# A channel MLP on one core: an inner Strassen level on four instead of two products of matmul 2, with seeded PSUM banks and weight sums kept in DRAM

## The chip, the cores and the metric

The kernel runs on one core of a Trainium2 chip. The metric is the device time of one execution in microseconds (us). Engines are named as in the profile: PE is TensorE (PEld its weight loads), DVE is VectorE, ACT is ScalarE, POOL is GpSimd, and SP is SyncE, whose queue issues nearly all DMAs.

## The reference

```python
B, S, D, F = 1, 2048, 1024, 3584          # all inputs bf16

def reference(x, w1, b1, w2, b2):
    y = _layernorm(x, axis=-1)            # (x - mean) / sqrt(var + 1e-5)
    h = _gelu(jnp.einsum("bsd,df->bsf", y, w1) + b1)    # tanh form
    return jnp.einsum("bsf,fd->bsd", h, w2) + b2
```

## The kernel before

The 2048 rows are done as two blocks (`s`) of 1024. A block is a layer norm of 8 tiles of 128 rows, a transposition into `yw_sb`, matmul 1 with the GELU into `h_sb`, and matmul 2 into the output.

Both matmuls use Strassen's algorithm in Winograd's form: operands are cut into 2 x 2 quarters, and seven products of sums of quarters take the place of eight. The sums of the left operand are called S1 to S4, those of the right T1 to T4, and the products 1 to 7: 1 is A11 B11, 2 is A12 B21, 3 is S4 B22, 4 is A22 T4, 5 is S1 T1, 6 is S2 T2, 7 is S3 T3. The result is C11 = 1 + 2; with U = 1 + 6: C12 = U + 5 + 3, C21 = U + 7 + 4 and C22 = U + 7 + 5. (The signs of the sums are chosen so that nothing but additions is left.)

**Matmul 1** (`mm1_unit`, L527) goes over 7 chunks of `w1` (three buffers in `w1_sb`), each of two units; a unit is 7 products of 4 matmuls with 512 columns (L548). The first chunk of the first block is done plainly (`mm1_plain`, L510), while x is still coming in. The w1 sums (L485) and the adds (`fin`, L565) are on DVE; copies of partial results (`snap`, L560) are on ACT or DVE; the GELU (L571) is on ACT. Output 11 of a unit is made as: product 1 is copied from its bank to SBUF (`o1`), product 2 goes to a bank of its own (`bp2`), DVE adds them (`c11`), ACT applies the GELU to the sum.

**Matmul 2** (`mm2_block`, L627) contracts over 28 tiles of 128, so a quarter of it has `NU` = 14. Products run in the order `SEQ2 = (1, 2, 5, 3, 6, 7, 4)`. A plain product (`prods`, L681) is 4 row tiles x 14 matmuls of 512 columns. Products 2 and 4 have a second Strassen level inside (`inner`, L733): seven sub-products of 14 matmuls with 256 columns, in the order 1, 5, 6, 2, 7, 3, 4, whose operand sums (8 per product, two DVE operations each) are written into space that is free then: `t1_sb` and `w1_sb` for product 2, `h` quarters 12 and 11 for product 4. All evictions of matmul 2 are DVE adds (L645), which add `b2` or an earlier result and leave a snapshot in `sn_sb` (12 slots) or an output tile in `o_sb`. The sums S1 to S4 and T1 to T4 of matmul 2 are made by DVE in each block (`sums`, L618): S over h quarters in place, T over the w2 quarters in place. The w2 quarters 11 and 21 lie in `w2a_sb`, 12 and 22 in `yw_sb`, where matmul 1's y operands were; they are loaded in each block.

**The order of work** is not written by hand. Each operation is an `Op` with a cost, dependencies, a due time (`prio`) and slots of a pool (8 PSUM banks, 12 snapshots, output buffers), and a planner (`Planner.place`, L101) places them on the engines one after the other: on each engine, among operations that can start within a small slack, the one with the earliest due time. This fixes the order in each engine's queue; on the chip the queues run in order and wait on semaphores. DMAs are planned as one server of 350 KB/us with 2.1 us of latency. The loads, output stores and the transposes by DMA (`dma_T`, L432) are issued on SP. The layer norm of block 1 (`ln`, L366) is statistics and scaling on DVE, with the power on POOL; three tiles of the head's layer norm run on ACT (`ln_act`, L383).

Of the kernel before, what the change touches and what calls it, by code (L numbers as in the profile page):

```python
# [6 lines left out]
ALU = mybir.AluOpType  # L7
# [16 lines left out]
P = 128  # L24
# [4 lines left out]
N_OUT = 6  # L29
N_WARM = 26  # L30
OPEN_JOBS = 5
LN_ACT = (2, 4, 6)
# [12 lines left out]
class Op:  # L45
    __slots__ = ("engs", "cost", "fn", "deps", "prio", "sem", "inc", "nbytes", "alloc", "frees", "eng", "start",
                 "end", "n", "order", "name", "waiting", "users", "slot", "ready")

    def __init__(self, engs, cost, fn, deps, prio, name, sem=None, inc=1, nbytes=None, alloc=None, frees=()):
        self.engs = (engs,) if isinstance(engs, str) else tuple(engs)  # L50
        self.cost, self.fn, self.prio, self.name = cost, fn, prio, name
        self.deps = [d for d in deps if d is not None]
        self.sem, self.inc, self.nbytes, self.frees = sem, inc, nbytes, frees
        self.alloc = () if alloc is None else alloc if isinstance(alloc, tuple) else (alloc,)
        self.eng = None
        self.start = self.end = 0.0
        self.n = 0
        self.slot = None


class Slots:

    def __init__(self, n):
        self.free = [(k, None) for k in range(n)]


class Holder:


    def __init__(self, pool):  # L70
        self.pool = pool
        self.k = None


class Planner:
# [13 lines left out]
    @staticmethod  # L89
    def take(alloc):  # L90

        n, res = {}, []
        for h in alloc:
            i = n.get(id(h.pool), 0)
            if i >= len(h.pool.free):
                return None
            res.append(h.pool.free[i])
            n[id(h.pool)] = i + 1
        return res

    def place(self):  # L101
# [12 lines left out]
        while left:  # L114
            best = None
            for e in self.ENGS:
                cands = []
                t0 = 1e9
                for o in avail:
# [6 lines left out]
                    for _, rel in slots:  # L126
                        if rel is not None:
                            r = max(r, rel.end + LAT)
# [15 lines left out]
            for h, (k, rel) in zip(o.alloc, self.take(o.alloc)):  # L144
                h.k = k
                if rel is not None:
                    o.deps.append(rel)
            for h in o.alloc:
                h.pool.free.pop(0)
# [8 lines left out]
            for h in o.frees:  # L158
                h.pool.free.append((h.k, o))
                h.pool.free.sort(key=lambda f: f[1].end if f[1] is not None else 0.0)  # L160
            order[e].append(o)
            for u in o.users:
                u.waiting -= 1
                u.ready = max(u.ready, o.end + (LAT if u.engs != (e,) else 0.06))
# [45 lines left out]
def bass_standalone__mixer_channel_mlp__prompt_kernel(  # L210
# [24 lines left out]
    with ExitStack() as es:  # L235
# [11 lines left out]
        b2_sb = sb("b2_sb", [P, D], BF16)  # L247
        b1r_sb = sb("b1r_sb", [FT, P], BF16)
# [23 lines left out]
        w2q = {11: w2a_sb[:, 0], 21: w2a_sb[:, 1], 22: quarter(yw_sb, 0), 12: quarter(yw_sb, 1)}  # L272
        w2q16 = {11: w2a16[:, 0], 21: w2a16[:, 1], 22: quarter(yw16, 0), 12: quarter(yw16, 1)}
# [13 lines left out]
        T_MM2 = TH * 5 * NU * MM512 + 2 * 7 * NU * MM256  # L287
# [30 lines left out]
        w2_ld = {}  # L318

        def load_w2(s, q, deps, prio):  # L320
            w2_ld[(s, q)] = dma(w2q[q], w2v[:, q // 10 - 1, :, (q % 10 - 1) * HT:(q % 10) * HT], deps, prio,
                                f"w2_{s}_{q}", f"w2_{q}", NU * P * HT * 2)


# [23 lines left out]
        def warm(n, deps, prio):  # L348
            hold = Holder(banks)
# [5 lines left out]
        hold_b = Holder(banks)  # L355
# [50 lines left out]

        y_in = {}
# [4 lines left out]
        def pe_T(s, i, prio):  # L412
            x_free[(s, i)], y_in[(s, i)] = [], []
            for k in range(2):
                hold = Holder(banks)
# [111 lines left out]
        def mm1_unit(s, c, v, T, t0):  # L527
# [3 lines left out]
            b0, bp2, bp5 = Holder(banks), Holder(banks), Holder(banks)  # L531
            hold = {1: b0, 6: b0, 7: b0, 4: b0, 5: bp5, 3: bp5, 2: bp2}
# [5 lines left out]
            def prod(p, deps):  # L538
# [4 lines left out]
                first = p in (1, 2, 5)  # L543
# [12 lines left out]
            def snap(p, o, hold_s, at):  # L556
                hb = hold[p]
                def fn(e):
                    src, dst = ps[:, hb.k, :], sn_sb[:, hold_s.k, :]
# [19 lines left out]
            o1 = snap(1, P1, s1, pt[6] - SLOT)  # L579
            P5 = prod(5, ())  # L580
            o5 = snap(5, P5, s5, pt[3] - SLOT)
            P6 = prod(6, (P1, o1))
            o2 = snap(6, P6, s2, pt[7] - SLOT)
            P2 = prod(2, ())
            c11 = fin(2, P2, o1, s1, pt[2] + 4 * SLOT, (bp2,))
            gelu(11, sn(s1), c11, pt[2] + 6 * SLOT, (s1,))
# [4 lines left out]
            c12 = fin(3, P3, o2, s2, pt[3] + 4 * SLOT, (bp5,))  # L591
# [10 lines left out]
        w2_free = {}  # L602
        SLOT2 = NU * MM512
        SEQ2 = (1, 2, 5, 3, 6, 7, 4)
        INNER = (2, 4)
        KI = NU // 2
        HI = HT // 2

        def sums(dst, a, b, op, deps, prio, name, step=2, cost=0.63):
# [3 lines left out]
            for g, k0 in enumerate(range(0, n, step)):  # L613
                k1 = min(k0 + step, n)
                dl = list(deps)
                for k in range(k0, k1):
                    dl += a[1][k] + b[1][k]
                o = add("DVE", cost * (k1 - k0) / step, lambda e, k0=k0, k1=k1: e.tensor_tensor(  # L618
                    out=dst[:, k0:k1, :], in0=a[0][:, k0:k1, :], in1=b[0][:, k0:k1, :], op=op),
                    list(dict.fromkeys(dl)), prio + 0.15 * step * g, f"{name}_{g}")  # L620
                res += [[o]] * (k1 - k0)
# [5 lines left out]
        def mm2_block(s):  # L627
            t0 = base2[s]
            pt = {}
            for p in SEQ2:  # L630
                pt[p] = t0
                t0 += 7 * NU * MM256 if p in INNER else TH * SLOT2
            m2, rd, sn = {}, {}, {}
            hb = [Holder(banks) for _ in range(TH)]
            h5 = [Holder(banks) for _ in range(TH)]
            hold = {1: hb, 6: hb, 7: hb, 5: h5, 3: h5}
            prev = {1: None, 5: None, 6: 1, 7: 6, 3: 5}
            A = {q: (h[q], [[h_ok[(s, q, u)]] for u in range(NU)]) for q in h}
            B = {q: (w2q[q], [[w2_ld[(s, q)]]] * NU) for q in w2q}

            def done(p):
                return m2[p] if p in INNER else [m2[(p, t)] for t in range(TH)]

            def plus(out, bank, x):
                return lambda e: e.tensor_tensor(out=out(), in0=bank(), in1=x(), op=ALU.add)  # L645

            def bias(d):
                return lambda: b2_sb[:, d * HT:(d + 1) * HT]

            def whole(t, h_):  # L650
                return lambda: t[:, h_.k, :]

            def keep(p, t, d, at):
                hs = sn[(p, t)] = Holder(snaps)
                rd[(p, t)] = add("DVE", 0.69, plus(whole(sn_sb, hs), whole(ps, hold[p][t]), bias(d)),
                                 (m2[(p, t)], b2_ld), at, f"r{p}_{s}_{t}", alloc=hs)

            def store(q, t, ho, deps, at):
                r = (s * NT + (q // 10 - 1) * TH + t) * P
                c = (q % 10 - 1) * HT  # L660
                add("SP", 0.42, lambda e: e.dma_start(of[r:r + P, c:c + HT], o_sb[:, ho.k, :]), deps, at + 0.5,
                    f"st{q}_{s}_{t}", sem=ho, inc=16, nbytes=P * HT * 2, frees=(ho,))

            def final(p, t, q, add_p, at, frees, kept=False):

                ho, hs = Holder(outs), sn[(add_p, t)]
                bank = whole(ps, hold[p][t])
                fn = [(plus(whole(o_sb, ho), bank, whole(sn_sb, hs)), ())]
                alloc = (ho,)
                if kept:  # L670
                    hk = sn[(p, t)] = Holder(snaps)
                    fn.append((plus(whole(sn_sb, hk), bank, bias(0)), ()))
                    alloc += (hk,)
                f = rd[(p, t)] = add("DVE", 0.65 * len(fn), fn, (m2[(p, t)], rd[(add_p, t)], b2_ld), at,
                                     f"o{q}_{s}_{t}", alloc=alloc, frees=(hs, *frees))
                store(q, t, ho, (f,), at)

            def prods(p, a, b):
                first = prev[p] is None
                for t in range(TH):  # L680
                    fn = [(lambda e, k=k, t=t: e.matmul(  # L681
                        ps[:, hold[p][t].k, :], lhsT=a[0][:, k, t * P:(t + 1) * P], rhs=b[0][:, k, :],
                        start=(first and k == 0), stop=(k == NU - 1), skip_group_check=True), a[1][k] + b[1][k])
                        for k in range(NU)]
                    dl = [] if first else [rd[(prev[p], t)]]
                    for _, dd in fn:
                        dl += dd
                    m2[(p, t)] = add("PE", NU * MM512, fn, list(dict.fromkeys(dl)), pt[p] + t * SLOT2, f"M{p}_{s}_{t}",
                                     alloc=hold[p][t] if first else None)
                    at = pt[p] + (t + 1) * SLOT2  # L690
                    if p in (1, 5, 6):
                        keep(p, t, 0 if p == 1 else 1, at)
                    if p == 6:
                        final(3, t, 12, 6, at + 1, (h5[t],))
                    if p == 7:
                        final(7, t, 22, 5, at, (hb[t],), kept=True)

            def inner(p, a, b, xb, yb, war, q, add_p):
# [6 lines left out]
                SUB = 2 * KI * MM256  # L705
                at = {r: pt[p] + k * SUB for k, r in enumerate(SEQ1)}

                def tt(dst, x, y, op, r, n):
                    return sums(dst, x, y, op, war, at[r] - 3 * SUB, f"i{n}_{nm}", step=4, cost=0.62)

                s1 = tt(xb[0], X["21"], X["22"], ALU.add, 5, "S1")
                t1 = tt(yb[0], Y["12"], Y["11"], ALU.subtract, 5, "T1")
                s2 = tt(xb[1], s1, X["11"], ALU.subtract, 6, "S2")
                t2 = tt(yb[1], Y["22"], t1, ALU.subtract, 6, "T2")
                s3 = tt(xb[2], X["11"], X["21"], ALU.subtract, 7, "S3")
                t3 = tt(yb[2], Y["22"], Y["12"], ALU.subtract, 7, "T3")
                s4 = tt(xb[3], X["12"], s2, ALU.subtract, 3, "S4")
                t4 = tt(yb[3], Y["21"], t2, ALU.subtract, 4, "T4")
# [191 lines left out]
```

## Time and profile before

| | |
|---|---|
| median of 6 runs | 353.19 us (351.96 to 353.67) |
| the profiled execution | 353.12 us |
| its span | 351.3 us, granted TensorE clock 1.00 |
| busy shares | PE 98%, DVE 81%, ACT 36%, PEld 53% |
| DMA | 40.98 MB, mean 117 GB/s |
| matmul 1 of block 0 | 29.65 to 99.6 us of the span (after the first chunk, done plainly) |
| matmul 2 of block 0 | 99.6 to 181 us |
| matmul 1 of block 1 | 181 to 266 us |
| matmul 2 of block 1 | 266 to 347.9 us |

The span is the time from the first to the last instruction in the profile; what the device time has beyond it lies ahead of it and behind. The profile comes from one execution. A line of the chain in order of time gives start, duration, engine, tile and source line, and the number of instructions; consecutive instructions of one line are merged. A few matmul records are missing from the trace, so a count can be low by some. In a line of the groups, "busy, mean" is followed by the idle time ahead of the instructions on their engine, with what ended it.

### The profile page before, as it was taken

How to read it: one execution, taken by the hardware profiler on the slowest of the kernel's cores; microseconds unless marked ns; L12 is line 12 of the kernel's file. 1: busy time of each engine (PE TensorE's matmuls, PEld its weight loads, DVE VectorE, ACT ScalarE, POOL GpSimd, SP SyncE). 2: the span in 40 equal slices, each digit the busy share in tenths (PEclk: the TensorE clock that was granted, in tenths of full speed). 3: DMA queues.
4: the chain of work that ended last, by engine and by line, in shares of the span. 5: the costliest groups of instructions: out<-in, count | busy, mean ns of one | idle time of the engine just before them, and what ended most of it. 6: DMA issues, size and time to landing. Idle time of an engine off the chain costs nothing.

```text
span 351.3 us, 5124 instructions
## 1 busy us (share of the span) xinstructions
PE 342.8 (98%) x2003; PEld 185.9 (53%) x2011; DVE 284.6 (81%) x509; ACT 124.9 (36%) x200; POOL 12.2 (3%) x31
## 2 busy tenths in 40 slices
PE   4999999999999999999999999999999999999996
PEld 4986444444445754444765444444444675444475
DVE  4688899798789998999997557656448999797993
ACT  3765766677630000000025677667763000000000
POOL 2220010001100000000000000000000000000000
PEclk9999999999999999999999999999999999999999
DMA  7648929700057057055656432130005701001101
GB/s 243 237 62 300 327 55 356 250 0 3 0 176 244 30 126 264 19 103 109 186 186 205 155 119 75 48 119 0 2 0 197 223 30 33 0 0 47 45 30 62
DMA packets 47394, 40.98 MB, mean 117 GB/s; under 512 B 12298, under 2 KB 45322, under 8 KB 47370
## 3 DMA queue, kind: packets, MB, share of 16 engines
q1 hardware_dynamic: 47226, 40.52, 37.6%
q8 instruction: 16, 0.26, 0.3%
q10 hardware_dynamic: 144, 0.13, 0.2%
q14 instruction: 8, 0.07, 0.1%
HBM read 33.82 MB, written 4.19 MB: 108 GB/s over the span
## 4 chain that ended last, share of the span: by engine, by line
PE 96%; DMA 1%; ACT 1%; SPq 0%; issue 0%; DVE 0%; DVEq 0%
PE ps L548 45%; PE ps L681 34%; PE ps L733 12%; PE ps L510 4%; DMA x_sb<-in_x_dram 1%; PE ps L416 1%; ACT h_sb L387 0%; SPq L293 0%; ACT yw_sb L423 0%; DVE o_sb L645 0%; DVEq L235 0%; ACT mv_sb L389 0%; PE ps L356 0%
## 5 line engine op out<-in xcount | busy, mean ns | idle before, releaser
L548 PE MATMUL ps<-yw_sb,t_sb 128*128 128x512 f16 x416 | 96.3, 379 | 0.0
L560 ACT COPY sn_sb<-ps 128x512 f32<-128x512 f32 x65 | 38.1, 587 | 102.7 <-PE ps L548 102.7
L548 PE MATMUL ps<-yw_sb,w_sb 128*128 128x512 f16 x312 | 73.9, 379 | 0.0
L681 PE MATMUL ps<-yw_sb,h_sb 128*128 128x512 f16 (+1 forms) x332 | 73.0, 379 | 0.2
L548 PEld LDWEIGHTS ps<-yw_sb,t_sb 128*128 128x128 f16 x416 | 40.7, 98 | 48.6
L565 DVE TENSOR_TENSOR sn_sb<-ps,sn_sb 128x512 f32<-128x512 f32 x78 | 52.5, 688 | 15.3 <-PE ps L548 14.7
L571 ACT ACTIVATE h_sb<-sn_sb,b_sb 128x512 f16<-128x512 f32 x78 | 55.2, 719 | 25.1 <-DVE sn_sb L565 21.0
L681 PEld LDWEIGHTS ps<-yw_sb,h_sb 128*128 128x128 f16 x336 | 32.8, 98 | 38.8
L548 PEld LDWEIGHTS ps<-yw_sb,w_sb 128*128 128x128 bf16 x312 | 30.4, 98 | 36.0
L681 PE MATMUL ps<-w2a_sb,h_sb 128*128 128x512 f16 (+1 forms) x220 | 48.5, 379 | 0.2
L618 DVE TENSOR_TENSOR h_sb<-h_sb 128x1024 f16<-128x1024 f16 x72 | 45.3, 669 | 0.0
L681 PEld LDWEIGHTS ps<-w2a_sb,h_sb 128*128 128x128 f16 x224 | 21.9, 98 | 26.4
L645 DVE TENSOR_TENSOR o_sb<-ps,sn_sb 128x256 bf16<-128x256 f32 (+1 forms) x48 | 23.0, 509 | 5.4 <-PE ps L733 4.5
L485 DVE TENSOR_TENSOR t_sb<-w_sb,t_sb 128x1024 f16<-128x1024 bf16 x26 | 17.9, 688 | 11.1 <-PE ps L548 9.0
L645 DVE TENSOR_TENSOR sn_sb<-ps,b_sb 128x512 f32<-128x512 f32 x32 | 22.0, 686 | 5.9 <-PE ps L681 5.7
L485 DVE TENSOR_TENSOR t_sb<-w_sb 128x1024 f16<-128x1024 bf16 x26 | 17.8, 683 | 9.4 <-DMA w_sb<-in_w_dram 5.1
L368 DVE BATCH_NORM_STATS2 st_sb<-x_sb 128x6 f32<-128x512 bf16 x26 | 17.2, 680 | 4.8 <-DMA x_sb<-in_x_dram 4.8
L571 ACT ACTIVATE h_sb<-ps,b_sb 128x512 f16<-128x512 f32 x26 | 17.7, 682 | 1.9 <-PE ps L548 1.9
L510 PE MATMUL ps<-yw_sb,w_sb 128*128 128x128 f16 x256 | 16.7, 227 | 0.8 <-ACT yw_sb L423 0.8
L733 PE MATMUL ps<-w2a_sb,h_sb 128*128 128x256 f16 (+1 forms) x140 | 16.9, 273 | 0.0
L510 PEld LDWEIGHTS ps<-yw_sb,w_sb 128*128 128x128 bf16 x256 | 15.8, 102 | 1.5 <-DMA w_sb<-in_w_dram 1.0
L733 PEld LDWEIGHTS ps<-w2a_sb,h_sb 128*128 128x128 f16 x140 | 13.7, 98 | 2.7
(54 smaller groups left out, 207.1 us busy)
## 6 DMA issues: line engine op xcount, KB each, us to landing
w_sb<-in_w_dram SPq DMA_DIRECT2D x28, 512.0 KB, 6.6
w2a_sb<-in_w_dram SPq DMA_DIRECT2D x4, 1792.0 KB, 8.7
yw_sb<-in_w_dram SPq DMA_DIRECT2D x4, 1792.0 KB, 9.8
out_dram<-o_sb SPq DMA_DIRECT2D x32, 128.0 KB, 1.8
x_sb<-in_x_dram SPq DMA_DIRECT2D x15, 256.0 KB, 7.6
yw_sb<-x_sb SPq DMA_TRANSPOSE x20, 2.5
b_sb<-in_b_dram SPq DMA_DIRECT2D x1, 256.0 KB, 6.4
x_sb<-in_x_dram ACTq DMA_DIRECT2D x1, 128.0 KB, 2.8
```

The source lines that it names most:

```text
L368: st = [add("DVE", 0.68, lambda e, k=k: e.bn_stats(st_sb[:, i, 6 * k:6 * k + 6], x_sb[:, i, k * HT:(k + 1) * HT]), (x_ld[(s, i)][k], *gate ...
L416: fn = [(lambda e, j=j, k=k, hold=hold: e.transpose(out=ps16[:, hold.k, j * P:(j + 1) * P], in_=x16[:, i, k * HT + j * P:k * HT + (j + 1) ...
L485: return add("DVE", 0.65, lambda e: e.tensor_tensor(out=tv(k), in0=x0, in1=x1, op=ALU.subtract), [*deps, *war.get(k, ())], prio + 0.5 * k, ...
L510: fn = [(lambda e, b=b, hb=hold[f], f=f, k=k, t=t: e.matmul(ps[:, hb.k, t * P:(t + 1) * P], lhsT=lhs[:, k, f * P:(f + 1) * P], rhs=yop[f"A ...
L548: fn = [(lambda e, k=k: e.matmul(ps[:, hold[p].k, :], lhsT=lhs[:, k, :], rhs=yop[yo][:, k, :], start=(first and k == 0), stop=(k == KH - 1 ...
L560: return e.copy(out=dst, in_=src) if o_.eng == "ACT" else e.tensor_copy(dst, src)
L565: return add("DVE", 0.69, lambda e: e.tensor_tensor(out=sn_sb[:, hold_s.k, :], in0=ps[:, hold[p].k, :], in1=sn_sb[:, hold_s.k, :], op=ALU. ...
L571: r = h_ok[(s, q, u)] = add("ACT", 0.70, lambda e: e.activation(out=h[q][:, u, :], in_=src(), func=ACT.Gelu_apprx_tanh, bias=b1_sb[:, f:f ...
L618: o = add("DVE", cost * (k1 - k0) / step, lambda e, k0=k0, k1=k1: e.tensor_tensor(out=dst[:, k0:k1, :], in0=a[0][:, k0:k1, :], in1=b[0][:, ...
L645: return lambda e: e.tensor_tensor(out=out(), in0=bank(), in1=x(), op=ALU.add)
L681: fn = [(lambda e, k=k, t=t: e.matmul(ps[:, hold[p][t].k, :], lhsT=a[0][:, k, t * P:(t + 1) * P], rhs=b[0][:, k, :], start=(first and k == ...
L733: fn = [(lambda e, k=k, j=j: e.matmul(ps[:, bank[r].k, j * HI:(j + 1) * HI], lhsT=x[0][:, k, j * P:(j + 1) * P], rhs=y[0][:, k, :], start= ...
```

## The change

- **Products.** Matmul 2 runs its products in the order 5, 1, 2, 6, 3, 7, 4, and products 1, 2, 3 and 4 have the inner level (two plain products of 56 matmuls with 512 columns become 98 matmuls with 256 columns in each block). The inner sums are one DVE operation of 7 x 256 elements each, and share buffers from product to product: a buffer is written again when the sub-product of the product before that read it is done.
- **Seeds.** ScalarE copies a sum or a bias into a PSUM bank first, and the matmuls accumulate onto it: the difference of the two halves of b2 (`dl_sb`) under product 5, b2 under the sub-products 1 and 5 of product 1, product 1's result under product 6 and under sub-product 2 of product 2, and so on. Many evictions turn from DVE adds into ACT copies; the others are DVE adds of 128 x 512.
- **Matmul 1.** From the third chunk of block 0 on (`fork`), product 1 is copied from its bank into another PSUM bank, onto which product 6 accumulates, and product 2 accumulates onto product 1's own bank. The add `c11` on DVE goes; the GELU of output 11 reads PSUM.
- **w2 sums.** T1 to T4 are made once, in matmul 1 of block 0, in seven groups: two raw pieces of 256 KB are loaded into the free `x_sb`, DVE makes the four sums, and four stores of 256 KB write them to a DRAM tensor (`w2_sums`). Matmul 2 of each block loads T1 to T4 from there into the slots A to D and an h quarter (H), each when what it held is done with. The load of T1 in block 0 waits for the whole preparation.
- **Layer norm of block 1.** All of its passes are on ACT, the small operations on POOL (`ln_act2`); x of block 1 is loaded when the preparation has left `x_sb`.
- The planner takes account of the time at which a matmul inside an operation needs its dependency, and can hand out contiguous groups of slots.

The core of the diff, cut:

```diff
+SEQ2 = (5, 1, 2, 6, 3, 7, 4)
+INNER = ((1, 2, 3, 4), (1, 2, 3, 4))
...
+            fork = n > 1
+            b1, b0, b5 = Holder(banks), Holder(banks, seeded=True), Holder(banks)
+            hold = {1: b1, 2: b1, 6: b0, 7: b0, 4: b0, 5: b5, 3: b5}
...
-            o1 = snap(1, P1, s1, pt[6] - SLOT)
+            o1 = snap(1, P1, b0 if fork else s1, pt[6] - SLOT)
...
-            P2 = prod(2, ())
-            c11 = fin(2, P2, o1, s1, pt[2] + 4 * SLOT, (bp2,))
-            gelu(11, sn(s1), c11, pt[2] + 6 * SLOT, (s1,))
+            P2 = prod(2, (o1,) if fork else ())
+            if fork:
+                gelu(11, lambda: ps[:, b1.k, :], P2, pt[2] + 4 * SLOT, (b1,))
...
+        def w2_prep(ldA, ldB, gate, prio, dt):
...
+            for g in range(NU // PU):
+                u = slice(g * PU, (g + 1) * PU)
...
+                ld = [dma(raw(e), w2v[:, e, u, HT:2 * HT], [*war(e), *gate], at + 0.1 * e, f"pw{g}_{e}", f"pw{base + e}",
+                          PU * P * HT * 2) for e in range(2)]
...
+                T1 = tt(0, raw(0), A11[:, u, :], (ld[0], ldB), at + 3)
+                T2 = tt(1, raw(1), t16(0), (ld[1], T1), at + 3.5)
+                T3 = tt(2, t16(1), A11[:, u, :], (T2, ldB, *war(2)), at + 4)
+                T4 = tt(3, A21[:, u, :], t16(1), (T2, ldA, *war(3)), at + 4.5)
+                for j, T in enumerate((T1, T2, T3, T4)):
+                    st = dma(tq[j, :, u, :], t16(j), (T,), at + 5 + 0.1 * j, f"ps{g}_{j}", f"ps{base + j}", PU * P * HT * 2)
...
+            def inner(p, a, b, xb, yb, war, O=None, bias=None, out=None, gate=()):
...
+                    return sums(dst, x, y, op, war.get((n[0], r), ()), at[r] - 3 * SUB, f"i{n}{r}_{nm}", step=KI)
...
+                sd = copy(lambda: bank_q(c2), lambda: quart(g, 0, 0), (ok[11], subs[1]), at[1], f"s2_{nm}", alloc=c2)
+                k1 = copy(lambda: sn_sb[:, kk.k, :], lambda: ps[:, c0.k, :], (subs[1],), end(1), f"k1_{nm}", alloc=kk)
+                k5 = dve(lambda e: plus(e, quart(g, 1, 1), bank_q(c5), quart(g, 1, 1)), (subs[5], ok[22]), end(5), f"k5_{nm}")
+                sub(6, (k1,))
+                k2 = dve(lambda e: plus(e, quart(g, 0, 1), bank_q(c0), quart(g, 0, 1)), (subs[6], ok[12]), end(6), f"k2_{nm}")
+                sub(2, (sd,))
...
+            M5 = plain(5, S1, B[5], h5, False, [(o,) for o in sd5])
...
+            g1, ok1, sub1 = inner(1, A[11], B[1], X0, Y0, war0, gate=(M5[2],), bias=(
+                b2_sb[:, None, 0:HI].to_broadcast([P, 2, HI]), e0_sb[:, None, :].to_broadcast([P, 2, HI])))
...
+            sub2 = inner(2, A[12], B[2], X0, Y0, war_of(sub1), O=(g1, okw), out=11)
...
+            M6 = plain(6, S2, B[6], hb, False, [(o,) for o in sdb])
...
+            sub3 = inner(3, S4, B[3], X0, Y0, war_of(sub2), O=(g12, {11: O12[1], 12: O12[1], 21: O12[3], 22: O12[3]}), out=12)
...
+            M7 = plain(7, S3, B[7], hb, False, [(o,) for o in O12])
...
-                if s == 0 and c == 2:
-                    for q in (11, 21):
-                        load_w2(0, q, (jobs[-1],), t0 + 20 * SLOT)
+                if s == 0 and c == 1:
+                    gate = (w1_use[0][-1],)
+                    t21 = load_w2(0, "A", "B21", gate, t0 + 20 * SLOT)
+                    t11 = load_w2(0, "B", "B11", gate, t0 + 20 * SLOT + 0.1)
+                    prep = w2_prep(t21[1][0][0], t11[1][0][0], gate, t0 + 22 * SLOT, 5.5)
+            if s == 0:
+                W = {5: load_w2(0, "A", "T1", prep, base2[0] - 10), 1: t11}
...
-                    load_x(s + 1, i, [*x_free[(s, i)], *(head_end if s == 0 else ())], base1[s] + 40 + i)
-                    ln(s + 1, i, base2[s] + 10 + 4 * i)
+                    load_x(s + 1, i, [*x_gate[i]], base2[s] - 4 + i)
+                    ln_act2(s + 1, i, base2[s] + 10 + 5 * i, wf["ring"])
```

## The prediction

> **What bounds the kernel now.** I read the busy shares, the chain that ended last in order of time, the waits, the stretches by window, then the timeline of VectorE (DVE) for the pace of its sums.
>
> ```profile
> PE 342.8 (98%) x2003; PEld 185.9 (53%) x2011; DVE 284.6 (81%) x509; ACT 124.9 (36%) x200; POOL 12.2 (3%) x31
> PEclk9999999999999999999999999999999999999999
> ```
>
> TensorE (PE) is busy for all but the first 8.6 us and the last 3.4 us of the span, at the full granted clock. The chain says whether it ever waits inside.
>
> ```profile
> 99.63 10.74 PE ps L681 x49
> ...
> 111.67 9.17 PE ps L733 x84
> 120.84 3.02 PE ps L681 x14
> 123.86 1.53 PE ps L733 x14
> ...
> 337.15 10.71 PE ps L733 x98
> 347.88 0.42 DVE o_sb L645
> ```
>
> The chain is matmuls (96%). Four times 14 matmuls 512 wide is a plain product: 4 x 3.02 = 12.08 us. 98 matmuls 256 wide is a product with an inner level: 7 x 1.53 = 10.71 us, also at the very end, where no other product could be slipped between its steps. So the inner level runs without a gap, and any matmul taken away is time taken away, as long as what feeds TensorE keeps up. What that leaves is in the windows (us; then busy us of PE, PEld, DVE, ACT, POOL; clock; DMA share; GB/s) and the waits.
>
> ```profile
> 29.65:64.00 34.35, 34.35 (x160) 15.54 (x159) 31.02 (x53) 23.43 (x38) 1.48 (x2) 1.00 0.81 268
> 64.00:99.60 35.60, 35.58 (x165) 16.17 (x165) 29.12 (x57) 24.21 (x39) 3.30 (x6) 1.00 0.12 38
> 99.58:181.00 81.42, 81.21 (x455) 44.69 (x458) 78.34 (x141) 3.39 (x6) 0.00 (x0) 1.00 0.54 152
> ACT sn_sb L560 <- PE ps L548: 102.7, 63, 77.1
> ```
>
> The first two are matmul 1 of block 0, the third matmul 2 of block 0. In matmul 2 VectorE is 96% busy, ScalarE (ACT) idles for 77.1 us at a stretch, and the DMA engines have room nearly everywhere but at the start of matmul 1.
>
> **TensorE's part.** Products 1 and 3 of each of two blocks go from 12.08 to 10.71 us: 4 x 1.37 = 5.48 us less, all on the path. No matmul is removed elsewhere (fork keeps seven products).
>
> At one place a page speaks against this. The Trainium skill ("TensorE: Matmul & The Clock Gate", Back-to-back issue gap) gives a sustained spacing of 81 ns for 128 columns and 131 ns for 512, set by weight load and matmul together. My estimate between them for 256 columns is 98 ns, so an inner level would cost 98 x 98 = 9.6 us against 56 x 131 = 7.3 us, and the change would lose 4 x 2.3 = 9 us. The rows above (216 and 109 ns) contradict it.
>
> **VectorE's part.** The timeline gives its pace back to back:
>
> ```profile
> 107.38 0.55 DVE L618 TENSOR_TENSOR w_sb<-w2a_sb 128x768 f16<-128x768 bf16 x1
> 107.84 0.69 DVE L618 TENSOR_TENSOR yw_sb<-yw_sb,w2a_sb 128x1024 f16<-128x1024 bf16 x1
> ...
> 135.74 4.29 DVE L618 TENSOR_TENSOR yw_sb<-yw_sb 128x1024 f16<-128x1024 bf16 x7
> ```
>
> Seven in 4.29 is 0.61 us for 1024 elements, and 0.46 us for 768 (107.38 to 107.84). The same slope gives an estimate of 1.05 us for the new 1792-wide inner sums and 1.2 us for 2048. Per block of matmul 2 after: inner sums 4 x 8 x 1.05 = 33.6; S1 to S4 4.3 + 3 x 4.2 = 16.9; 28 evictions of 128x512 x 0.65 = 18.2. Sum 68.7 us, in block 0 about 7 us more for y sums and w1 sums, of 79 us; before it was 78.3 of 81.4. T1 to T4 leave it (28 x 0.61 = 17 us a block) and come back once, in matmul 1 of block 0, where the layer norm of the next rows (8 x 2.2 us there and in matmul 2) and the final add of output 11 (10 units x 0.69) leave. So VectorE has a little more room in the mean. The order matters more: between the first use of a free operand buffer (product 1's fifth sub-product done, some 15 us into the block) and the last chunk of S3 (59 us) I count some 40 us of VectorE work in 43.5.
>
> Inside an inner level three steps have only one sub-product (1.53 us) to cover an eviction: 6 after 1, 7 after 6, 4 after 7. That is 24 places. An eviction of 0.69 us (DVE) or 0.59 us (ACT, the L560 copy) and some 0.2 us of hand-over (an estimate, the planner's own PE_LAT) leave 0.64 us; what they can run into is an operation just begun, 1.2 us where the longest was 0.69. The cost is between nothing (the last inner level of before, with evictions of 0.76 us, has none) and 24 x 0.56 = 13 us. I take 0.9 us, near the lower end, because that row is the same chain under a fuller VectorE.
>
> **ScalarE's part.** 29 copies a block x 0.59 = 17 us. PSUM as destination is not in the trace; bounds are 0.59 (this copy) and 0.69 us (the GELU), and less is not excluded. The layer norm of block 1 adds, from the rows of its three tiles in the head, 1.06 + 0.19 + 0.20 + 1.15 + 0.19 us and one more pass, by an estimate 1.1: 8 x 3.9 = 31 us, each queued ahead of later seeds if its x is late; x lands some 6 us into the block, where no seed is due before 10 us. Both lie in the 77 us in which ScalarE waits now. Without that cover an activation of 1.15 us ahead of a seed costs at most 0.5 us, which is in the bounds above. The table is loaded once now, with these functions in use; no reload is added. Fork: the o1 copy was already a condition of product 6; the add c11 between product 2 and its GELU goes, a PSUM bank is held 2 to 3 us longer in its place. Product 2 waits for o1 too, but product 6 ahead of it on TensorE waits for the same copy. Nothing on the path.
>
> At the head of matmul 2, product 5 needs S1, and S1 the last GELU of matmul 1: GELU 0.69, sum 0.69 and hand-overs are some 2 us after the last product, and the matmuls that use that piece stand 12 x 0.216 = 2.6 us into the first tile. The seeds of tiles 3 and 4 wait for the same GELU and have 6 us. Behind them waits all of TensorE, so cover that is gone costs what is missing, up to 1 us a block by these numbers; I take none.
>
> **DMA's part.** Matmul 2 starts with product 5 now, whose T1 comes from DRAM, and its load waits for the whole preparation. The stretch before 99.6 must carry: four w1 chunks 4.2 MB, B21 and B11 3.7, raw pieces 3.7, stores of T1 to T4 7.3, T1 back 1.8: 20.7 MB. Rates, from three windows:
>
> ```profile
> 33.00:35.00 2.00, 2.00 (x11) 0.92 (x10) 1.84 (x4) 0.85 (x2) 0.00 (x0) 1.00 1.05 396
> 57.00:59.00 2.00, 2.00 (x11) 0.88 (x9) 1.90 (x4) 0.76 (x2) 0.00 (x0) 1.00 1.09 356
> x_sb<-in_x_dram SPq DMA_DIRECT2D x15, 256.0 KB, 7.6
> w2a_sb<-in_w_dram SPq DMA_DIRECT2D x4, 1792.0 KB, 8.7
> ```
>
> About 350 GB/s with weights in 1 KB rows, 390 with x in 2 KB rows (as the stores are). B11 is in at 30.7 + 4.7 MB / 350 GB/s = 44. A group (of seven) moves 0.52 MB in and 1.05 out, and w1 takes its share: 1.5 + 2.7 + 1.3 = 5.5 us. The last stores are down at 44 + 6 x 5.5 + 8 (four sums shared with matmul 1's work, a store) = 85, T1 8.7 us later at 94: 6 us ahead of product 5, at no cost. The prepared sums stand in VectorE's queue behind their loads, and the final adds of matmul 1 behind them; today's longest such wait costs TensorE nothing:
>
> ```profile
> DVE t_sb L485 <- DMA w_sb<-in_w_dram: 6.9, 6, 2.5
> ```
>
> The cover is gone when a group takes over 6.5 us. Stores of this size at full load are not in the trace: a group is between 5.5 us and (7.6 + 1.2 + 7.6) / 2 = 8.2 us, two groups being in flight and each landing at the loaded x load's 7.6. I take 5.5 to 6.5, as 7.6 us was measured behind a queue of weights. SP issues 42 more DMAs there, at some 0.5 us 21 us of 45; w1 loads queued behind a waiting store have two chunks (24 us) of cover.
>
> The Trainium skill ("DMA: Bandwidth & Descriptors", Measured) asks for 1 MiB a transfer, with 341 GB/s there and 138 at 64 KB; my estimate at 256 KB is 240, by which T1 would come some 12 us later and the gain be gone. The 256 KB loads in the first window above ran at 396.
>
> Inside matmul 2 five quarters of 1.8 MB, 2.1 MB of x and 3.1 MB of w1 are 14.4 MB in 79 us, half of the rate. The tightest is B21, issued as today's yw_sb load at the block's start (9.8 us to landing) for sums that can't start before 15 us. The sixteen transposes of the next rows can start 34 us into the block and hold SP 1.3 us each, as today; the loads of T3 and T4 that queue between them are needed from 56 us on, 20 us after T3's slot comes free and 10 after T4's. Nothing.
>
> At the end one add of 0.69 us replaces two (0.76), one 256 KB store two of 128 KB: nothing.
>
> **Sum.** The profiled execution took 353.12 us (span 351.3, 1.82 around it; the median of the runs is 353.19). 353.12 - 5.48 + 0.9 = 348.5.
>
> **Rivals.** (1) The steps of the inner levels wait: at 0.15 to 0.25 us in each of 24 places, 3.6 to 6 us, the time is 351.3 to 353.6. For it: longer sums, longer activations, 40 us of work in 43.5. Against it: the gapless 10.71 us. (2) Slower: preparation isn't done when product 5 starts. From 6.5 us a group TensorE stands at 99.6, 6 us for each us more; from 7.4 the gain is gone; at 8.2 the stall is 10 us and the time 359. For it: seven groups of load, four sums and four stores through two buffers, all queues in order. Against it: the DMA share of 0.12 from 64 to 99.6.
>
> **Chances.** Forecast 0.62, at 347.4 to 351; the first rival 0.16; the second 0.22. A measurement of this kernel tells about 0.3% (1.06 us) from no change. Faster 0.62 + 0.06 = 0.68, same 0.10, slower 0.22. The range starts at 347.2 (all of 5.48 and the runs' scatter) and must reach into the second rival: to 355.0, a stall of 6.5 us, about 7.5 us a group; beyond lie 0.14. The forecast's own range is 347.4 to 351.
>
> **What would show it.** Matmuls: 224 fewer of 512 columns, 392 more of 256. Right: product 5 begins within 0.3 us of 99.6 and each block of matmul 2 takes 79 to 80 us, down from 81.8. Wrong: TensorE waiting for a DMA of w2 at 99 us (second rival), or for ps copies and sums inside product 1, 2 or 3 (first rival).

## The result and the profile after

The changed kernel takes 351.07 us (median of 22 runs, 349.56 to 352.96), the kernel before 353.17 us (45 runs); the ratio is 0.9945, 95% interval 0.9933 to 0.9957. That is 1.9 us (1.5 to 2.4) faster, where 4.6 us were forecast (353.12 to 348.5). The profiled execution took 350.42 us, its span is 348.7 us.

The page of the changed kernel, busy shares and the two rows that changed most:

```profile
PE 338.2 (97%) x2179; PEld 201.1 (58%) x2179; DVE 253.1 (73%) x355; ACT 183.0 (52%) x304; POOL 21.7 (6%) x47
DMA  7639999999948661669996540330003766105301
GB/s 255 229 62 293 348 356 347 294 383 334 351 179 314 211 212 45 122 165 223 287 358 211 191 122 9 111 120 2 0 0 123 301 212 211 33 30 175 128 32 60
```

VectorE went from 81 to 73%, ScalarE from 36 to 52%, and the DMA engines are full from 26 to 96 us (slices of 8.7 us), the whole of matmul 1 of block 0. The chain in order of time, first through block 0, then block 1 (steps under 0.1 us left out):

```profile
35.05 12.09 DMA x_sb<-in_w_dram
47.16 0.70 DVE x_sb L711
47.88 5.28 DMA w_sums<-x_sb
53.18 6.45 DMA x_sb<-in_w_dram
...
64.73 7.12 DMA x_sb<-in_w_dram
...
75.36 25.21 PE ps L603 x116
100.57 12.09 PE ps L786 x56
...
161.82 4.24 DMA yw_sb<-x_sb
166.17 0.70 DVE yw_sb L503
...
186.51 79.52 PE ps L603 x368
266.03 12.09 PE ps L786 x56
278.11 16.81 PE ps L832 x154
```

Before, the chain was matmuls from 8.6 us on. Now it leaves TensorE in block 0: it runs through the raw loads and prepared sums (L711) in matmul 1, and through transposes and y sums (L503) in matmul 2. From 186.51 us on it is matmuls alone. By windows, matmul 2 of block 0, matmul 1 of block 1 and matmul 2 of block 1:

```profile
100.57:186.51 85.94, 84.67 (x585) 56.73 (x584) 69.99 (x85) 46.84 (x81) 14.04 (x24) 1.00 0.74 212
186.51:266.03 79.52, 79.52 (x369) 35.87 (x368) 45.07 (x68) 54.91 (x87) 0.00 (x0) 1.00 0.25 80
266.03:345.12 79.09, 79.05 (x560) 54.62 (x558) 60.54 (x71) 16.10 (x29) 0.00 (x0) 1.00 0.39 137
```

Block 1 is as forecast: 79.09 us against 81.8 before, two times 1.37 less, and no idle time on TensorE. Block 0 is not: TensorE is idle there. The chain comes back to matmul 1 of block 1 without a break at 186.51 us, where it was 186.59 before: all that block 0 should have saved is gone. TensorE's own waits in those stretches, first matmul 1, then matmul 2:

```profile
PE ps L603 <- DVE sn_sb L621: 0.7, 2, 0.4
PE ps L832 <- ACT ps L770: 0.7, 1, 0.7
PE ps L832 <- DVE w2a_sb L678: 0.6, 1, 0.6
```

The profile models matmul ends, so these are short by some tenths of a microsecond. I measure a **gap** as the distance between the starts of two successive matmuls beyond 216 ns (512 columns) or 109 ns (256). The gaps are 0.5 us at 61 and at 75 us (with a small one 1.1 us together), 0.85 us at 149, and 0.86 us at 173 to 180 us; with one of 0.08 us, 2.9 us in all.

### The profile page after: what moved, and what is told of

It is laid out like the page before. It is cut to its first block, busy times and chain, and to the rows that moved or that the text cites. A ratio compares the mean times of both kernels' runs of the same rounds, so it can differ in the third digit from the quotient of the medians.

```text
span 348.7 us, 5466 instructions
## 1 busy us (share of the span) xinstructions
PE 338.2 (97%) x2179; PEld 201.1 (58%) x2179; DVE 253.1 (73%) x355; ACT 183.0 (52%) x304; POOL 21.7 (6%) x47
## 4 chain that ended last, share of the span: by engine, by line
PE 76%; DMA 11%; DVE 6%; SPq 4%; issue 1%; ACT 1%; DVEq 0%
PE ps L603 32%; PE ps L832 21%; PE ps L786 17%; DMA x_sb<-in_w_dram 7%; PE ps L561 4%; SPq L483 2%; SPq L322 2%; DMA w_sums<-x_sb 2%; DVE x_sb L711 1%; DMA x_sb<-in_x_dram 1%; DMA yw_sb<-x_sb 1%; DVE h_sb L678 1%; PE ps L467 1%; DVE w2a_sb L678 1%; DVE t_sb L678 1%
## 5 line engine op out<-in xcount | busy, mean ns | idle before, releaser
L603 PEld LDWEIGHTS ps<-yw_sb,w_sb 128*128 128x128 bf16 x312 | 30.3, 98 | 36.3 <-ACT ps L616 0.6
L627 ACT ACTIVATE h_sb<-sn_sb,b_sb 128x512 f16<-128x512 f32 x54 | 38.2, 718 | 24.6 <-DVE sn_sb L621 22.8
L786 PE MATMUL ps<-w2a_sb,h_sb 128*128 128x512 f16 x224 | 49.6, 379 | 0.0
L770 ACT COPY sn_sb<-ps 128x512 f32<-128x512 f32 x30 | 17.5, 582 | 53.5 <-DVE o_sb L750 41.5
L678 DVE TENSOR_TENSOR h_sb<-h_sb 128x1024 f16<-128x1024 f16 (+2 forms) x42 | 38.6, 951 | 2.1 <-ACT h_sb L627 2.1
L627 ACT ACTIVATE h_sb<-ps,b_sb 128x512 f16<-128x512 f32 x50 | 34.1, 684 | 7.6 <-PE ps L603 6.7
L750 DVE TENSOR_TENSOR o_sb<-ps,sn_sb 128x512 bf16<-128x512 f32 x32 | 21.9, 688 | 14.4 <-PE ps L832 8.4
L832 PE MATMUL ps<-w_sb,t_sb 128*128 128x256 f16 x252 | 30.0, 273 | 0.0
L832 PEld LDWEIGHTS ps<-w_sb,t_sb 128*128 128x128 f16 x252 | 24.6, 98 | 3.3
L786 PE MATMUL ps<-yw_sb,h_sb 128*128 128x512 f16 x112 | 24.8, 379 | 0.0
L832 PE MATMUL ps<-w2a_sb,h_sb 128*128 128x256 bf16 (+1 forms) x182 | 22.0, 273 | 1.3 <-ACT ps L770 0.7
L750 DVE TENSOR_TENSOR sn_sb<-ps,sn_sb 128x512 f32<-128x512 f32 x24 | 16.4, 685 | 7.7 <-PE ps L832 4.2
L770 ACT COPY ps<-sn_sb 128x512 f32<-128x512 f32 x14 | 8.1, 587 | 26.0 <-PE ps L832 22.2
```

The lines of the kernel that those rows point to most:

```text
L603: fn = [(lambda e, k=k: e.matmul(ps[:, hold[p].k, :], lhsT=lhs[:, k, :], rhs=yop[yo][:, k, :], start=(first and k == 0), stop=(k == KH - 1 ...
L627: r = h_ok[(s, q, u)] = add("ACT", 0.70, lambda e: e.activation(out=h[q][:, u, :], in_=src(), func=ACT.Gelu_apprx_tanh, bias=b1_sb[:, f:f ...
L678: o = add("DVE", cost2(w * dst.shape[-1]), lambda e, k0=k0, k1=k1: e.tensor_tensor(out=dst[:, k0:k1, :], in0=a[0][:, k0:k1, :], in1=b[0][: ...
L750: plus = lambda e, out, x, y: e.tensor_tensor(out=out, in0=x, in1=y, op=ALU.add)
L770: return act(lambda e: e.copy(out=out(), in_=src()), deps, at, name, **k)
L786: fn = [(lambda e, k=k, t=t: e.matmul(ps[:, banks_[t].k, :], lhsT=a[0][:, k, t * P:(t + 1) * P], rhs=b[0][:, k, :], start=(first and k == ...
```

## The experiments

**Theory Q (queues):** each gap is an instruction that is ready but stands behind one that waits, in an in-order queue; the planner put it there because it took a load, GpSimd or a transpose to be quicker than it is. **Theory I (inner level):** the steps of the inner levels are too tight for their evictions. Further rivals stand in the expectations. Most experiments change only what the planner believes, so the work is the same and only the order in the queues differs. The planner then places everything anew, so such an edit can change the order in other places too.

| run | median us | ratio to before, 95% | gaps in matmul 1 | ahead of product 5 | product 2 or 3 | product 4 | T1 lands, us |
|---|---|---|---|---|---|---|---|
| changed kernel (22 runs) | 351.07 | 0.9945 (0.9933 to 0.9957) | 1.1 | 0 | 0.85 | 0.86 | 99.4 |
| after_again | 350.65 | 0.9949 (0.9929 to 0.9969) | 1.9 | 0 | 0.85 | 0.9 | 99.6 |
| pw_late | 349.94 | 0.9922 (0.9897 to 0.9946) | 0 | 1.8 | 1.1 | 0.1 | 101.4 |
| pool_cost | 349.93 | 0.9916 (0.9890 to 0.9941) | 2.4 | 0 | 0.17 | 0.7 | 100.5 |
| yt_late | 349.69 | 0.9914 (0.9887 to 0.9940) | 2.6 | 0 | 0 | 0 | 99.9 |
| x_after_T1 | 350.26 | 0.9928 (0.9904 to 0.9952) | 2.4 | 0 | 0 | 1.4 | 97.0 |
| no_pw2 | 349.30 | 0.9908 (0.9881 to 0.9936) | 0 | 0 | 0 | 1.5 | 95.2 |
| nofork | 348.14 | 0.9845 (0.9828 to 0.9863) | 0.25 | 0 | 0.38 | 0.15 | 100.8 |
| all_orders | 348.72 | 0.9884 (0.9858 to 0.9910) | 0 | 1.1 | 0 | 0.1 | 100.8 |
| all_x | 347.21 | 0.9823 (0.9807 to 0.9839) | 0 | 0 | 0 | 0.1 | 98.4 |
| best | 347.27 | 0.9826 (0.9811 to 0.9842) | 0 | 0 | 0.17 | 0 | 94.3 |
| all_x_nofork | 347.29 | 0.9850 (0.9824 to 0.9876) | 0 | 0 | 0 | 0.1 | 98.4 |

The gaps are those of one profiled execution each, all in block 0 (some have one of 0.08 to 0.16 us more at its end). That execution is not a typical one: in ten of the twelve rows it is slower than the row's median, by 0.15 to 1.5 us, so a row's gaps and its median do not add up. From the start of the last matmul of the plain first chunk to the modelled end of the last matmul of the kernel, less the gaps, I get 312.9 us in each of the twelve profiles with the change, and 318.4 us before. So TensorE's saving is 5.5 us in all of them, and the gaps, the head and 0.2 us at the very end are the whole difference between them.

**The kernel again.** No edit.

> The changed kernel once more, unaltered, beside the three variants below. Theory Q (queues): of the 5.48 us saved on TensorE some 2.8 us are given back in block 0 alone, in four gaps of TensorE: two in matmul 1 (0.5 us each, near 61 and 75 us; VectorE's add waits behind a prepared sum whose raw load is late), one near 149 us (0.85 us; a seed on ScalarE waits behind a layer norm pass that waits for GpSimd) and one near 173 us (0.75 us; an inner sum on VectorE waits behind a y sum that waits for transposes). The gaps should come again at the same places, 2 to 4 us in sum, none in block 1, and the ratio to before 0.993 to 0.996. Theory I (inner level): the steps of the inner levels are too tight everywhere; then gaps move about and block 1 has some as well. Theory T (T1 late): product 5 of block 0 waits for T1 in some executions, as it landed only 1.15 us ahead in the profile; then a gap at 100 us may show.

The same four gaps at the same places, 3.8 us in sum; matmul 1's were 1.9 us where they were 1.1, in the same order of instructions. The raw load issued at 53.1 us took 6.9 us to land, where it took 6.5 us in the first profile, and TensorE was 0.4 us earlier. So part of the spread of the runs is how late the loads are. That the median (351.07) lies above the first profiled execution (350.42) fits it, but the other runs have no trace.

**Raw loads planned later.**

```diff
-                o.end = dma_free + DMA_FIX
+                o.end = dma_free + DMA_FIX + next((v for n, v in {'pw': 2.0}.items() if o.name.startswith(n)), 0.0)
```

> Only the planner's idea of the raw loads of the preparation is changed: it takes them to land 2 us later, so the prepared sums go further back in VectorE's queue. Same work, same data. Theory Q: the two gaps near 61 and 75 us go (1.1 us), and T1 lands at or after the start of product 5, which may give up to 1 us back at 100 us; the other two gaps stay: 0.990 to 0.995 of before. Theory I: gaps of the inner levels are unchanged and matmul 1 has the same loss: no change against the unaltered kernel.

As Q has it: both gaps of matmul 1 are gone with the same work. In the changed kernel VectorE's queue around the first of them reads (start, duration, engine, line, tile, shape, in brackets idle time and what ended it):

```profile
59.65 0.69 DVE L711 TENSOR_TENSOR x_sb<-x_sb,w2a_sb 128x1024 f16<-128x1024 bf16 x1 [0.95 <-DMA x_sb<-in_w_dram]
60.45 0.69 DVE L711 TENSOR_TENSOR x_sb<-x_sb 128x1024 f16<-128x1024 bf16 x1
61.06 0.69 DVE L621 TENSOR_TENSOR sn_sb<-ps,sn_sb 128x512 f32<-128x512 f32 x1
```

and TensorE's queue:

```profile
61.80 1.04 PE L603 MATMUL ps<-yw_sb,t_sb 128*128 128x512 f16 x4 [0.37 <-DVE sn_sb L621]
```

The add at 61.06 frees a bank for product 4 and stood behind two prepared sums, the first of which waited for its load. But the price moved: T1 came at 101.4 us, and TensorE waited for it in front of product 5:

```profile
101.43 2.76 PE L786 MATMUL ps<-w2a_sb,h_sb 128*128 128x512 f16 x12 [1.65 <-DMA w2a_sb<-w_sums]
```

The prediction's second rival (preparation not done in time) is real, at 1.8 us, as soon as the sums go back in the queue. A gap at 127 us (0.98 us) is new: again a layer norm pass on ScalarE that waits for GpSimd, in another place.

The two other gaps, which Q had expected to stay, did not: 0.11 us is left near 150 us, and 0.1 us at product 4. At product 4 the edit had changed the order as well: the first three inner sums now stand ahead of the y sums (so they do in the runs pool_cost and nofork). This run shows that matmul 1's gaps come from the order; it does not tell the other two apart.

**GpSimd's operations at their slow times.**

```diff
-            vp = add("POOL", 0.2, lambda e: e.tensor_scalar(
+            vp = add("POOL", 0.6, lambda e: e.tensor_scalar(
...
-            rs = add("POOL", 0.6, lambda e: e.tensor_tensor(
+            rs = add("POOL", 1.2, lambda e: e.tensor_tensor(
...
-            nb = add("POOL", 0.3, lambda e: e.tensor_tensor(
+            nb = add("POOL", 0.9, lambda e: e.tensor_tensor(
```

> Only the planner's costs of the three small GpSimd operations of the layer norm of block 1 are changed (0.2, 0.6 and 0.3 us become 0.6, 1.2 and 0.9, as they took in the slow instances), so a layer norm's last pass stands behind the seed of product 3 in ScalarE's queue. Theory Q: the gap near 149 us (0.85 us) goes and the rest stays: 0.7 to 1 us below the unaltered kernel. Theory I: the seed and the copy k1 themselves are too slow for their step; the gap stays at 0.5 us or more.

The gap at 149 us went from 0.85 to 0.17 us; the others stayed, matmul 1's at 2.4 us in this execution and product 4's at 0.7 us. ScalarE's queue in the changed kernel, then in this one:

```profile
148.10 1.24 ACT L454 ACTIVATE x_sb<-x_sb,st_sb,rstd_sb 128x1024 f16<-128x1024 bf16 x1 [1.71 <-POOL st_sb L451]
149.25 0.57 ACT L770 COPY ps<-sn_sb 128x512 f32<-128x512 f32 x1
```

```profile
149.94 0.59 ACT L770 COPY ps<-sn_sb 128x512 f32<-128x512 f32 x1 [5.20 <-PE ps L832]
150.47 0.58 ACT L770 COPY sn_sb<-ps 128x512 f32<-128x512 f32 x1
150.94 1.24 ACT L454 ACTIVATE x_sb<-x_sb,st_sb,rstd_sb 128x1024 f16<-128x1024 bf16 x1
```

In the first, the seed (L770, into PSUM) stands behind the layer norm's last pass (L454), which idled 1.71 us for GpSimd. In the second the seed goes first and waits only for its own sub-product.

**Transposes planned later.** The same edit as for the raw loads, with `{'yt1': 4.0}`.

> Only the planner's idea of the DMA transposes of block 1's y is changed (4 us later), so the y sums stand behind the first inner sums of product 4 in VectorE's queue. Theory Q: the gap near 173 us (0.75 us) goes, the rest stays: 0.6 to 0.9 us below the unaltered kernel. Theory I: the gap stays, as VectorE has too much to do for product 4 in any order.

The gap at 173 us is gone, and the one at 149 as well, which Q had not forecast (the next run has the same and tells why); matmul 1's gaps were 2.6 us. VectorE's queue in the changed kernel, then in this one:

```profile
166.17 1.29 DVE L503 TENSOR_TENSOR yw_sb<-yw_sb 128x1024 f16<-128x1024 f16 x2 [1.71 <-DMA yw_sb<-x_sb]
167.38 1.08 DVE L678 TENSOR_TENSOR h_sb<-h_sb 128x1792 f16<-128x1792 f16 x1
```

```profile
165.62 1.08 DVE L678 TENSOR_TENSOR h_sb<-h_sb 128x1792 f16<-128x1792 f16 x1
166.62 1.08 DVE L678 TENSOR_TENSOR w2a_sb<-h_sb 128x1792 f16<-128x1792 f16 x1
```

The transposes that the y sums wait for stand behind the load of T4 (`h_sb<-w_sums`). SyncE's queue in the changed kernel:

```profile
149.00 3.82 SPq L483 DMA_TRANSPOSE yw_sb<-x_sb  x3
152.87 0.58 SPq L322 DMA_DIRECT2D h_sb<-w_sums  x1
153.49 7.65 SPq L483 DMA_TRANSPOSE yw_sb<-x_sb  x4
161.19 0.58 SPq L779 DMA_DIRECT2D out_dram<-o_sb  x1
161.82 1.22 SPq L483 DMA_TRANSPOSE yw_sb<-x_sb  x1
```

The three ahead of the load took 1.3 us each on SyncE, the four behind it 1.9 us, and the last one landed 4.2 us after it was issued (161.82 in the chain), where the median is 2.5 us. No run takes T4's load away, so how much of this is its doing stays open.

Theory I falls with these three: the same evictions and sums in the same steps leave no gap of more than 0.2 us once the one late instruction is out of the way. The three runs' medians lie 0.7 to 1 us below the kernel again, but their intervals overlap it; the verdict rests on the gaps.

**x behind T1.**

```diff
-                    load_x(s + 1, i, [*x_gate[i]], base2[s] - 4 + i)
+                    load_x(s + 1, i, [*x_gate[i], *prep], base2[s] - 4 + i)
```

> The changed kernel with one edit: the loads of block 1's x stand behind T1's load in SP's queue instead of partly ahead of it. Theory Q: T1 lands 2 to 4 us earlier, but nobody waits for it here, so the four gaps stay and the time is that of the unaltered kernel within 0.5 us (0.993 to 0.996 of before). Theory T (in the unprofiled executions T1 is what comes late): 1 us or more below the unaltered kernel.

T1 landed 2.4 us earlier, the time is the changed kernel's within its interval: T1 is not what made the unprofiled executions slow. The gap at 149 us was absent in this execution too, with the seed behind the same pass (L454). The pass began 0.65 us after product 3's first sub-product (148.31 against 147.66), in the changed kernel 2.13 us after it (148.10 against 145.97). In the run before, and in the next one, it was 0.65 us as well. So this wait costs TensorE something or nothing by where ScalarE and TensorE stand to each other, and a difference of 1.5 us decided it.

**Without the raw loads.**

```diff
-                ld = [dma(raw(e), w2v[:, e, u, HT:2 * HT], [*war(e), *gate], at + 0.1 * e, f"pw{g}_{e}", f"pw{base + e}",
-                          PU * P * HT * 2) for e in range(2)]
+                ld = [[*war(e), *gate] for e in range(2)]
...
-                T1 = tt(0, raw(0), A11[:, u, :], (ld[0], ldB), at + 3)
-                T2 = tt(1, raw(1), t16(0), (ld[1], T1), at + 3.5)
+                T1 = tt(0, A21[:, u, :], A11[:, u, :], (*ld[0], ldA, ldB), at + 3)
+                T2 = tt(1, A21[:, u, :], t16(0), (*ld[1], ldA, T1), at + 3.5)
```

> The 14 loads of raw w2 pieces are left out (3.7 MB); the prepared sums are made from B21 and B11, which are in SBUF already, so T1 to T4 are not the right ones. Theory Q: no prepared sum waits for a load; matmul 1 of block 0 has no gap, T1 lands 4 to 8 us earlier; the gaps at 149 and 173 us stay at about 0.8 us each: 0.989 to 0.993 of before. Theory D (VectorE is too full in matmul 1 with 28 more sums, whatever the loads do): the gaps near 61 and 75 us stay.

No gap in matmul 1 with all 28 prepared sums still in VectorE's queue: the loads made the gaps, not the amount of work on VectorE. Product 4's gap stayed and was larger (1.5 us); the one at 149 us was absent, against the expectation.

**Without the fork.**

```diff
-            fork = n > 1
+            fork = n > 99
```

> The fork of matmul 1 is undone: product 1 is copied to SBUF, product 2 has its own bank and VectorE adds the two, as before the change; all else as changed. Theory Q: TensorE never waits for that add in block 1, so block 1 stays without gaps; in block 0 VectorE has 10 x 0.69 us more beside the prepared sums, and the two gaps of matmul 1 grow by up to 1 us together: 0.994 to 0.998 of before. Theory F (fork pays by itself): matmul 1 of block 1 gets longer by 1 us or more.

A miss: it was faster than the changed kernel, 0.9845 against 0.9945, and not slower. The gaps say why. Matmul 1's are 0.25 us where they were 1.1 to 2.6, and those at products 3 and 4 are smaller too: with ten adds more, VectorE comes to most of the prepared sums later, when their loads are in. VectorE's waits for raw loads in matmul 1, changed kernel first:

```profile
DVE x_sb L711 <- DMA x_sb<-in_w_dram: 6.5, 4, 4.3
```

```profile
DVE x_sb L711 <- DMA x_sb<-in_w_dram: 1.9, 2, 1.2
```

(The longest of each, 4.3 and 1.2 us, is that of the very first sum, near 48 us, where TensorE has no gap.) Whether the fork costs anything by itself is told by the last run below.

**The three reorderings together.** All three edits above, with `{'pw': 2.0, 'yt1': 4.0}`.

> The three reorderings, with the x loads ahead of T1 as in the changed kernel. Theory Q: no gap in matmul 1 nor at 149 and 173 us, but T1 lands at about 101.4 us as in the run with the raw loads planned later, so one gap of 1 to 2 us stands ahead of product 5: 0.986 to 0.990 of before. If there is none, the place of the x loads wasn't what made T1 late.

**The same, with x behind T1.**

> The three reorderings together (raw loads planned 2 us later, transposes 4 us later, the GpSimd operations at 0.6, 1.2 and 0.9 us), and the loads of block 1's x issued behind T1's load instead of ahead of it (1.8 MB, at 390 GB/s 4.7 us of DMA time). Theory Q: no gap in matmul 1, none near 149 and 173 us; T1 still waits for the last store and lands at 99 to 100 us, so the gap ahead of product 5 is 0 to 0.7 us: 0.985 to 0.990 of before. Theory I: the gaps of the inner levels come up elsewhere, and the time stays at 0.991 or more.

**The same, with T1's load in two parts.** The core of the edit, cut:

```diff
...
+        def load_T1(cut, deps, prio):
+            res = []
+            for j, (k0, k1) in enumerate(((0, cut), (cut, NU))):
+                g0, g1 = k0 // PU, k1 // PU
+                o = dma(w2q16["A"][:, k0:k1, :], tq[0][:, k0:k1, :], [*t4s[g0:g1], *tq_ok[0][g0:g1], *deps], prio - 10 * (1 - j),
...
-                W = {5: load_w2(0, "A", "T1", prep, base2[0] - 10), 1: t11}
+                W = {5: load_T1(8, (), base2[0] - 10), 1: t11}
```

> As the last one, and the load of T1 in block 0 is split: units 0 to 7 are loaded when groups 0 to 3 of the preparation are done, units 8 to 13 when the rest is, each waiting only for the stores of T1 and the sums that read slot A. Theory Q: T1 is there by 97 us, product 5 starts without a wait, and all of TensorE's saving is kept: gaps under 0.5 us in sum, 0.984 to 0.988 of before (5.48 us would be 0.9845). Theory I: 0.990 or more.

With the three orders alone only the gap ahead of product 5 is left (1.1 us). Moving 1.8 MB of x behind T1 closes it, and the kernel takes 347.21 us, 0.9823 of before. Its chain has no step outside TensorE between the head and the end; in block 0:

```profile
29.50 69.93 PE ps L603 x324
99.43 12.09 PE ps L786 x56
111.52 16.81 PE ps L832 x154
```

T1 landed at 98.4 us, 1.1 us ahead; splitting it puts it at 94.3 and changes nothing more. The span of this version is 5.7 us shorter than before's, 5.5 of which is TensorE's saving. Its ratio makes 5.7 to 6.8 us, more than the run had been expected to bring; the tenths beyond I leave open.

**All of it without the fork.** Both edits.

> The version with all reorderings and the x loads behind T1, with the fork of matmul 1 undone (VectorE adds products 1 and 2 again, 24 x 0.69 us more on VectorE). Theory Q: fork moves no gap by itself once no prepared sum waits for its load; the time is that of the version with fork, 0.981 to 0.985 of before. Theory F (fork costs time by itself, as the faster run without it suggests): faster than the version with fork by 0.5 us or more. Theory F' (fork gives room that matmul 1 needs): slower by 0.5 us or more, with gaps in matmul 1.

Spans of 345.5 and 345.6 us, medians of 347.29 and 347.21 us, intervals that just overlap: the fork is worth nothing that can be measured here. The gain of the run without it came from the order on VectorE.

## Why the prediction was wrong

The direction and TensorE's term were right, the size was wrong: the sum gave back 0.9 us of 5.48. The profile shows 2.9 us given back, the medians 3.5 us; the 0.6 us between the two stay open but for what is said of the spread.

**Right.** 5.48 us on TensorE: 5.5 measured. The estimate from the Trainium skill's spacing ("TensorE: Matmul & The Clock Gate", Back-to-back issue gap; its 131 ns for 512 columns, my 98 ns for 256 between its 81 and 131) fell, as the rows of before said: 216 and 109 ns here too. VectorE's load in matmul 2: 60.5 us in block 1 for an estimate of 68.7 (part of S1 and two of the 32 inner sums are made ahead of the window, and an inner sum takes 1.00 us for 1.05). Seeds at 0.57 to 0.59 us: at the lower bound. The transfer rate: 293 to 383 GB/s in the eight full slices of the page, 338 in the mean, a little under the estimate's 350 to 390, in a mix of pieces of 256 KB, 512 KB and 1.8 MB. The estimate of 240 GB/s for 256 KB pieces from the Trainium skill ("DMA: Bandwidth & Descriptors", Measured) is not what these runs show; the section's table is of transfers issued from GpSimd, and these are issued on SyncE, many in a queue.

**The step that failed.** The 0.9 us were put on the 24 tight steps of the inner levels. These cost nothing: block 1 has 12 of them and no gap, and block 0 has none once the queues are reordered (the run all_x). TensorE did wait for a PSUM copy inside product 3, the sign that the prediction had named for its first rival, but that copy was held up in its queue and not too long for its step. The loss came from three covers that I had named and priced at nothing or at 0.5 us:

- "[T]oday's longest such wait costs TensorE nothing": I took a wait of 2.5 us for harmless because one such wait had been. The prepared sums wait for their raw loads with the adds of matmul 1 behind them; this cost 1.1 to 2.6 us. The raw loads landed 6.5 us after issue (the median), on DMA engines that were full from 26 us on; before, these were free from 70 us on.
- "Without that cover an activation of 1.15 us ahead of a seed costs at most 0.5 us": I counted the activation's length and not what it may itself wait for. It waited 1.71 us for GpSimd, and the gap was 0.85 us (0.98 us at another place in one other run).
- "The sixteen transposes ... Nothing": I looked at what stands behind the transposes in SP's queue (T3 and T4), not at what a late transpose holds up elsewhere. T4's 1.8 MB went out ahead of the last transposes, the y sums waited for these, and behind the y sums stood the inner sums of product 4: 0.6 to 1.4 us in the runs that have this gap.

**Nearly wrong: T1.** I had it 6 us ahead of product 5; it was 1.15 us ahead (99.4 against 100.57), and only because matmul 1 had itself been held up. A group took 6 us (first sums of groups 0 and 5 at 47.2 and 77.0 us) for my 5.5, and the load of T1 stood behind several loads of x, which I left out of the 20.7 MB. That T1 cost nothing here was luck: the second rival was closer than I had it, and TensorE waited 1.8 and 1.1 us for T1 in the two runs in which matmul 1's delay was gone and x still stood ahead of T1 (pw_late, all_orders).

## What to carry to other kernels

When an engine is bound and work is taken from it, price not only the operations that feed it but each one that now *waits* in an in-order queue: ask what it waits for at worst, and who stands behind it. A wait that costs nothing today is no bound for one on a transfer that will run on full DMA engines. Where queues are ordered by a planner, telling it how late things come (here 2 us more for a load, 4 for a transpose, two to three times as much for GpSimd's small operations) was, with the x loads moved behind T1, worth more than the change itself had brought: 347.2 us against 351.1, with the same work.

## What the runs showed of the hardware

**GpSimd beside VectorE.** The layer norm's 128x1 operations on GpSimd (L448, L451) took 0.55 and 0.19 us alone, and up to 1.43 and 1.16 us beside VectorE's sums. The timeline of the changed kernel, GpSimd first, then VectorE:

```profile
142.58 1.16 POOL L451 TENSOR_TENSOR st_sb<-mv_sb,rstd_sb 128x1 f32<-128x1 f32 x1
```

```profile
142.62 1.08 DVE L678 TENSOR_TENSOR t_sb<-h_sb 128x1792 f16<-128x1792 f16 x1
```

The operation of 1.16 us ended at 143.75, 0.05 us after the sum on VectorE (142.62 to 143.70). The same 0.05 us stands at 106.52, 119.89 and 141.54. Beside an add with one operand in PSUM (L750, at 132.5 us) the same operations took 0.55 and 0.19 us. The Trainium skill ("SBUF — State Buffer", Who interferes with whom) has the rule: a VectorE instruction with two inputs in SBUF contends with a GpSimd instruction that reads SBUF, for a pair of ports that one of them holds alone; one with at most one SBUF input, outside the two-port modes, does not. The trace agrees for a GpSimd operation that starts during a sum. One that started first (0.55 us at 146.75, the sum of 1.23 us at 146.78) shows no delay of either. Of the 1.71 us that ScalarE waited ahead of the gap at 149 us, this accounts for some 0.5 us: GpSimd's last operation there took 0.68 us for 0.19. The change made these sums longer (1.08 to 1.22 us for 0.69) and put GpSimd's chain in front of ScalarE's queue; I had not looked this up, and it was a rule against the change.

**The clock in the head.** Four of the thirteen profiles have a stretch at half the granted clock in the head (the clock row of the changed kernel's page has an 8 in its second slice). In three it lasted 3.4 us, and no loss shows: their plain first chunks ended at 29.1 to 29.5 us, those of the profiles without one at 29.5 to 30.1 us. In the run without the fork it lasted 6.8 us, and the plain first chunk ended at 30.8 us, 1.3 us later than in the changed kernel's profile. The mean granted clock of that execution is 0.990. Of the changed kernel's 22 executions four are at 0.988 to 0.990, and they took 352.05 to 352.96 us, where the median of the other 18 is 350.85 us. So this is likely a part of the spread; it is not shown, as these four have no trace. It is no part of the accounting above, which starts behind it.
